# A softplus whose VectorE operations keep one operand in the matmul's PSUM bank

## The chip, the cores and the metric

The kernel runs on one core of a Trainium2 chip. The metric is the device time of one execution in microseconds (us). The engines have their own in-order instruction queues: TensorE (PE, its weight loads PEld), VectorE (DVE), ScalarE (ACT), GpSimd (POOL) and SyncE (SP). Data lies in SBUF and in eight PSUM banks, each as large as one 128 x 512 float32 tile.

## The reference

Three layers follow one another on 24576 rows (8 batches of 3072) of 256 channels: a long convolution by FFT, a first layer of 8 experts with a fixed capacity for each, and a dense second layer. The change touches the activation of the second layer alone:

```
h = x @ w_in                                        # 24576 x 256 by 256 x 2048
g = np.maximum(h, 0.0) + np.log1p(np.exp(-np.abs(h)))
return (g @ w_out).astype(np.float32)               # by 2048 x 256
```

The kernel keeps float32 accuracy: it writes each operand of a matmul as a high part, rounded to the type that the matmul reads (`F32R`), and a low part, the rest. For the same reason the logarithm is not taken as it stands. With a = exp(-|h|) and u = 1 + a rounded to float32, log1p(a) is ln(u) + (a - (u - 1)): the last term gives back what the rounding of u lost, to first order.

## The kernel before

About the first 700 us are the convolution and the first piece of the routing. After it one stage holds both layers and the rest of the routing. The 24576 rows are cut into 48 groups of 512 rows, six for each expert, and the stage is a list `seq` of steps that is written out by hand: a step of kind "m" is `moe1(i, f)`, one 128-wide slice of the expert's hidden layer, a step of kind "s" is `sp1(i, f)`, one 128-wide slice f of the second layer, called a block below. A group has 8 m steps and 16 s steps, and they alternate as m, s, s. The recording order is the order on each engine; no scheduler moves anything.

In each step PE does 12 matmuls of 128 x 512: six for the step's own product into a fresh PSUM bank (`bank()`, the tile `work`), then six of an earlier step's second product (`moe2` two steps later, `sp2` four steps later), which add up in four more banks `y` and `o`. So four banks are left for `work`, and these also take transposes and the small matmuls of the routing.

A block goes through several engines. `sp1` records on ACT a = |h| (L982), a = exp(-a) (L983), l = ln(1 + a) (L986); on DVE p = max(h, 0) + a (L984) and a = (a + 1) - 1 (L987); on POOL l = l - a (L989). `join`, called within the next step, adds p to l on DVE (L997), and `split`, called within the step after, rounds the sum to gh on ACT (L1004) and subtracts it on POOL to get gl (L1006). Of the m steps the names are hh (ACT, L949) and hl (DVE, L950). The bank of a block is last read by p; a, p and l lie in SBUF, three buffers each.

DVE has a second job. `Router` decides which row goes to which expert, one expert at a time (a phase), while the groups of the expert before are computed. `advance` records a piece of it at the head of a step, ahead of the step's own DVE work: preparing keys (L171 to L202), 16 rounds of a bisection, each with three counting passes over 1536 columns (L220) and a few operations on 3 columns (L223, L229, L232), and index lists at the end (L366 to L396). A phase takes 144 steps, six times 24. After the last phase the groups run without routing. The weights of the next expert are split by L788 and L793 on DVE. POOL issues the indirect DMAs (L766, L775, L918, L1047).

## Time and profile before

| | |
|---|---|
| time, median of 3 runs | 4475.76 us (4472.63 to 4477.92) |
| profiled execution, span | 4480.6 us |
| busy share PE / DVE / ACT / POOL | 92% / 88% / 57% / 65% |
| chain that ended last, by engine | DVE 42%, PE 42%, POOL 5%, issue 4%, ACT 3% |

The profiled execution is given by its span, from the first to the last instruction; it lies 4.8 us above the median of the three timed runs. Two engines share the chain evenly. The span has to be read by stages: in the page's 40 slices DVE is at eight or nine tenths from the eighth to the 32nd and at six to eight behind that, where the routing is over and PE is at nine to the last but one.

### The profile page before, as it was taken

What the parts mean: (1) busy time and instruction counts of PE and PEld (TensorE: products, weight loads), DVE (VectorE), ACT (ScalarE), POOL (GpSimd) and SP (SyncE); (2) the same over time, 40 slices, a digit from 0 to 9 for tenths busy, and PEclk for the clock granted to TensorE, in tenths of its full rate; (3) what the DMA queues carried; (4) which work ended last, traced back from release to release, by engine and by line L of the source; (5) the groups of instructions that cost most, each with busy time, mean ns of one, the idle gap of its engine ahead of it and who ended that gap; (6) DMA issues with size and microseconds to landing.
All of it is one profiled execution on the core that took longest, in us unless ns stands there. A gap on an engine that the chain in (4) does not pass through costs nothing.

```text
span 4480.6 us, 57930 instructions
## 1 busy us (share of the span) xinstructions
PE 4109.7 (92%) x19372; PEld 3273.8 (73%) x19372; DVE 3940.3 (88%) x6302; ACT 2575.1 (57%) x4749; POOL 2932.6 (65%) x2627
## 2 busy tenths in 40 slices
PE   8999888889889988899889988998889999999998
PEld 7898766667666766677667766776667788778886
DVE  6999666999999899999999999999998987787776
ACT  4565554445555555555555655565555666666665
POOL 3444334557666776677666866777668777887776
PEclk9999989999999999999999999999999999999999
DMA  9888660000000010000000000001000000000000
GB/s 270 260 256 245 189 170 27 10 12 24 29 13 16 20 32 15 10 24 28 16 16 11 29 26 11 17 20 34 12 10 25 23 20 14 24 27 14 20 12 12
DMA packets 226491, 228.87 MB, mean 51 GB/s; under 512 B 19376, under 2 KB 183600, under 8 KB 226192
## 3 DMA queue, kind: packets, MB, share of 16 engines
q1 hardware_dynamic: 195056, 144.25, 11.3%
q0 software_dynamic: 26528, 72.53, 5.1%
q10 hardware_dynamic: 4608, 8.39, 0.6%
q8 instruction: 153, 2.51, 0.2%
q14 instruction: 146, 1.20, 0.1%
HBM read 125.74 MB, written 93.85 MB: 49 GB/s over the span
## 4 chain that ended last, share of the span: by engine, by line
DVE 42%; PE 42%; POOL 5%; issue 4%; ACT 3%; DMA 2%; DVEq 0%; SPq 0%; another core or an unknown queue 0%; ACTq 0%; POOLq 0%
PE work L976 11%; PE o L1018 11%; DVE U L220 10%; DVE l L997 6%; PE work L945 6%; PE y L960 6%; DVE a L987 5%; DVE p L984 4%; POOL l L989 3%; DVE hl L950 2%; PE bank L669 2%; DVE c L232 2%; PE bank L583 1%; PE pair L604 1%; DVE U L202 1%
## 5 line engine op out<-in xcount | busy, mean ns | idle before, releaser
L989 POOL TENSOR_TENSOR l<-l,a 128x512 f32<-128x512 f32 x768 | 1135.3, 1478 | 617.6 <-DVE a L987 591.5
L1006 POOL TENSOR_TENSOR gl<-l,gh 128x512 fp32r<-128x512 f32 x760 | 1002.5, 1319 | 404.9 <-ACT gh L1004 399.5
L976 PE MATMUL work<-yh,WI 128*128 128x512 f32 x3072 | 876.7, 407 | 57.6 <-DVE hl L950 38.3
L1018 PE MATMUL o<-gh,WO 128*128 128x512 f32 x3072 | 869.9, 404 | 64.9 <-DVE oT L1023 39.0
L1004 ACT CAST gh<-l 128x512 fp32r<-128x512 f32 x768 | 473.1, 616 | 751.2 <-DVE l L997 744.5
L997 DVE TENSOR_TENSOR l<-l,p 128x512 f32<-128x512 f32 x768 | 743.4, 968 | 69.0 <-POOL l L989 65.6
L976 PEld LDWEIGHTS work<-yh,WI 128*128 128x128 f32 x3072 | 567.7, 191 | 268.1 <-DVE hl L950 63.3
L1018 PEld LDWEIGHTS o<-gh,WO 128*128 128x128 f32 x3072 | 585.1, 192 | 229.4 <-DVE oT L1023 48.6
L987 DVE TENSOR_SCALAR a<-a 128x512 f32<-128x512 f32 x768 | 606.0, 789 | 140.3 <-ACT l L986 75.8
L982 ACT ACTIVATE a<-work 128x512 f32<-128x512 f32 x768 | 452.6, 589 | 322.1 <-PE work L976 311.6
L220 DVE TENSOR_SCALAR_CACHE_REDUCE U<-U,c 128x1536 bf16<-128x1536 uint16 x336 | 607.6, 1808 | 12.7 <-DMA raw<-w_in 7.1
L984 DVE SCALAR_TENSOR_TENSOR p<-work,a 128x512 f32<-128x512 f32 x768 | 525.0, 684 | 98.0 <-ACT a L983 91.6
L1018 PE MATMUL o<-gl,WO 128*128 128x512 f32 x1536 | 499.2, 406 | 48.4 <-POOL gl L1006 31.2
L986 ACT ACTIVATE l<-a 128x512 f32<-128x512 f32 x768 | 483.9, 630 | 36.4 <-ACT a L983 1.8
L976 PE MATMUL work<-yl,WI 128*128 128x512 f32 x1536 | 497.2, 404 | 5.5 <-DVE yl L967 4.4
L983 ACT ACTIVATE a<-a 128x512 f32<-128x512 f32 x768 | 485.7, 632 | 24.4
L949 ACT ACTIVATE hh<-work 128x512 fp32r<-128x512 f32 x384 | 229.4, 597 | 366.3 <-PE work L945 364.9
L945 PE MATMUL work<-xh,wring 128*128 128x512 f32 x1536 | 433.5, 404 | 4.3 <-DVE p L984 4.1
L960 PE MATMUL y<-hh,wring 128*128 128x512 f32 x1536 | 430.6, 403 | 0.0
L1018 PEld LDWEIGHTS o<-gl,WO 128*128 128x128 f32 x1536 | 287.4, 191 | 148.0 <-POOL gl L1006 55.5
L976 PEld LDWEIGHTS work<-yl,WI 128*128 128x128 f32 x1536 | 293.8, 191 | 85.5 <-DVE yl L967 14.4
L960 PEld LDWEIGHTS y<-hh,wring 128*128 128x128 f32 x1536 | 296.1, 193 | 73.3
(233 smaller groups left out, 6018.0 us busy)
## 6 DMA issues: line engine op xcount, KB each, us to landing
x<-x SPq DMA_DIRECT2D x96, 256.0 KB
a_cols<-a SPq DMA_DIRECT2D x96, 256.0 KB
A<-a_cols SPq DMA_DIRECT2D x64, 384.0 KB
y_rows<-yo SPq DMA_DIRECT2D x128, 192.0 KB
f_late<-U SPq DMA_DIRECT2D x72, 192.0 KB
YT<-f_late SPq DMA_DIRECT2D x72, 192.0 KB
U<-U SPq DMA_DIRECT2D x48, 96.0 KB
raw<-moe_w_in ACTq DMA_DIRECT2D x16, 256.0 KB
```

The source lines that it names most:

```text
L220: V.tensor_scalar(s, R, c3[:, k:k + 1], 0.0, op0=OP.is_ge, op1=OP.add, accum_out=cnt[:, k:k + 1])
L945: nc.tensor.matmul(b, w[:, wh, k], xx[i][:, k], start=(n == 0), stop=(n == 5))
L960: nc.tensor.matmul(Yb[i][m], w[:, 1, wh, m * 128:(m + 1) * 128], hx, start=(f == 0 and n == 0), stop=(f == 7 and n == 2))
L976: nc.tensor.matmul(b, WI[:, wh, k, f * 128:(f + 1) * 128], yy[i][:, k], start=(n == 0), stop=(n == 5))
L983: nc.scalar.activation(a, a, AF.Exp, scale=-1.0)
L984: nc.vector.scalar_tensor_tensor(p, b, 0.0, a, op0=OP.max, op1=OP.add)
L986: nc.scalar.activation(l, a, AF.Ln, bias=1.0)
L987: nc.vector.tensor_scalar(a, a, 1.0, -1.0, op0=OP.add, op1=OP.add)
L989: nc.gpsimd.tensor_tensor(l, l, a, op=OP.subtract)
L997: nc.vector.tensor_tensor(l, l, p, op=OP.add)
L1006: (nc.vector if i == NT - 1 and f % 2 else nc.gpsimd).tensor_tensor(gl, l, gh.bitcast(F32), op=OP.subtract)
L1018: nc.tensor.matmul(Ob[i][m], WO[:, wh, f, m * 128:(m + 1) * 128], gx, start=(f == 0 and n == 0), stop=(f == 15 and n == 2))
```

## The change

The tile p is gone, a tile u takes its place. ACT writes u = 1 + a and takes the logarithm of u. All VectorE work of the block moves into `join`: three operations, of which the first two write their result into the block's PSUM bank, and the third, into SBUF, reads it from there. First h becomes max(h, 0) + ln(u), then (u - 1) minus that, then a minus that: the same sum, ln(u) + max(h, 0) + (a - (u - 1)). POOL loses its subtraction and keeps gl.

```diff
             a = wk.tile([128, 512], F32, name="a", bufs=3)
-            p = wk.tile([128, 512], F32, name="p", bufs=3)
+            u = wk.tile([128, 512], F32, name="u", bufs=3)
             l = wk.tile([128, 512], F32, name="l", bufs=3)
             nc.scalar.activation(a, b, AF.Abs)
             nc.scalar.activation(a, a, AF.Exp, scale=-1.0)
-            nc.vector.scalar_tensor_tensor(p, b, 0.0, a, op0=OP.max, op1=OP.add)
+            nc.scalar.activation(u, a, AF.Identity, bias=1.0)
             split(0)
-            nc.scalar.activation(l, a, AF.Ln, bias=1.0)
-            nc.vector.tensor_scalar(a, a, 1.0, -1.0, op0=OP.add, op1=OP.add)
+            nc.scalar.activation(l, u, AF.Ln)
             join(0)
-            nc.gpsimd.tensor_tensor(l, l, a, op=OP.subtract)
-            joins.append((i, f, l, p))
+            joins.append((i, f, b, a, u, l))
...
         def join(keep):
             while len(joins) > keep:
-                i, f, l, p = joins.pop(0)
-                nc.vector.tensor_tensor(l, l, p, op=OP.add)
+                i, f, b, a, u, l = joins.pop(0)
+                nc.vector.scalar_tensor_tensor(b, b, 0.0, l, op0=OP.max, op1=OP.add)
+                nc.vector.scalar_tensor_tensor(b, u, -1.0, b, op0=OP.add, op1=OP.subtract)
+                nc.vector.tensor_tensor(l, a, b, op=OP.subtract)
                 parts.append((i, f, l))
```

The line numbers of the changed kernel are u = 1 + a L984, the logarithm L986, and L995, L996, L997 for the three operations of `join`; L1004 and L1006 stay gh and gl.

On DVE, in a bisection of a routing phase (the end of one round and the start of the next, where a group of 512 rows ends and the next begins; U is the routing's scratch, c its thresholds), these rows stood:

```order
L220 TENSOR_SCALAR U_21895,cnt<-U_21785,c_22009 128x1536
L223 SCALAR_TENSOR_TENSOR low<-rconst,c_22009 128x3
L984 SCALAR_TENSOR_TENSOR p<-work,a 128x512
L987 TENSOR_SCALAR a<-a 128x512
L997 TENSOR_TENSOR l<-l,p 128x512
L950 SCALAR_TENSOR_TENSOR hl<-work,hh 128x512
L997 TENSOR_TENSOR l<-l,p 128x512
L933 TENSOR_TENSOR xl<-work,xh 128x512 x2
L229 TENSOR_SCALAR ge,n<-work 128x3
L232 SCALAR_TENSOR_TENSOR c_22133<-n,low 128x3
L220 TENSOR_SCALAR U_21895,cnt<-U_21785,c_22133 128x1536
```

and these stand at the same place now:

```order
L220 TENSOR_SCALAR U_21893,cnt<-U_21785,c_22007 128x1536 x2
L223 SCALAR_TENSOR_TENSOR low<-rconst,c_22007 128x3
L995 SCALAR_TENSOR_TENSOR work<-work,l 128x512
L996 SCALAR_TENSOR_TENSOR work<-u,work 128x512
L997 TENSOR_TENSOR l<-a,work 128x512
L950 SCALAR_TENSOR_TENSOR hl<-work,hh 128x512
L995 SCALAR_TENSOR_TENSOR work<-work,l 128x512
L996 SCALAR_TENSOR_TENSOR work<-u,work 128x512
L997 TENSOR_TENSOR l<-a,work 128x512
L933 TENSOR_TENSOR xl<-work,xh 128x512 x2
L229 TENSOR_SCALAR ge,n<-work 128x3
L232 SCALAR_TENSOR_TENSOR c_22133<-n,low 128x3
```

The two operations of a block's own step (p and a) are gone, and the three of `join` stand where L997 alone stood, in the next step: the first of two s steps in a row records none of this on DVE any more.

On ACT, the rows of an m step and the two s steps behind it stood so (the last row is the next m step's):

```order
L949 ACTIVATE hh<-work 128x512
L1004 CAST gh<-l 128x512
L982 ACTIVATE a<-work 128x512
L983 ACTIVATE a<-a 128x512
L1004 CAST gh<-l 128x512
L986 ACTIVATE l<-a 128x512
L982 ACTIVATE a<-work 128x512
L983 ACTIVATE a<-a 128x512
L986 ACTIVATE l<-a 128x512
L949 ACTIVATE hh<-work 128x512
```

and so now:

```order
L949 ACTIVATE hh<-work 128x512
L1004 CAST gh<-l 128x512
L982 ACTIVATE a<-work 128x512
L983 ACTIVATE a<-a 128x512
L984 ACTIVATE u<-a 128x512
L1004 CAST gh<-l 128x512
L986 ACTIVATE l<-u 128x512
L982 ACTIVATE a<-work 128x512
L983 ACTIVATE a<-a 128x512
L984 ACTIVATE u<-a 128x512
L986 ACTIVATE l<-u 128x512
```

Each s step has one operation more (L984), ahead of the logarithm. The order on PE is unchanged.

One more thing moves. The pool of the four `work` banks gives a new tile the bank that was given back first in the recorded order. Before, that made the banks take turns, each new tile taking that of the fourth tile before it, for each of the 1543 tiles but the first four. A block now gives its bank back after the third operation of `join`, a step later, and the built program has other pairs: 32 of its tiles take the bank of a block two steps back or two and a half (15 that of a first s block, 17 that of a second one), and another 48, which are transposes in the main, that of a first s block two and a half steps back. All others wait for a block's bank from three to five steps back, or for one that something else held.

## Rows read from the trace of the kernel before

**Rows 1.** Page, part 1: busy us (share of the span), instructions of each engine.

```profile
PE 4109.7 (92%) x19372; PEld 3273.8 (73%) x19372; DVE 3940.3 (88%) x6302; ACT 2575.1 (57%) x4749; POOL 2932.6 (65%) x2627
```

**Rows 2.** Windows over a 144-step phase: busy us of PE, PEld, DVE, ACT, POOL; clock.

```profile
2519.00:2598.00 79.00, 70.93 (x303) 54.37 (x301) 77.15 (x101) 46.74 (x87) 60.88 (x50) 1.00 0.12 34
2598.00:2849.00 251.00, 222.02 (x928) 171.11 (x928) 238.74 (x357) 138.60 (x243) 164.86 (x137) 0.97 0.05 15
2849.00:2925.00 76.00, 71.90 (x326) 56.90 (x326) 71.03 (x128) 45.06 (x78) 54.19 (x44) 1.00 0.04 15
2925.00:2999.00 74.00, 73.23 (x339) 57.55 (x339) 65.31 (x124) 45.56 (x79) 59.92 (x51) 1.00 0.08 26
```

**Rows 3.** Windows, 24 steps behind the last phase, same columns.

```profile
4100.00:4169.00 69.00, 69.00 (x306) 55.65 (x305) 53.76 (x63) 44.54 (x79) 52.83 (x44) 1.00 0.05 16
```

**Rows 4.** Lines in 2519 to 2999: xcount, busy us, mean ns, idle before, its releasers.

```profile
L989 POOL TENSOR_TENSOR l<-l,a 128x512 f32<-128x512 f32 x96 | 142.6, 1486 | 83.5 <-DVE a L987 80.8 <-DVE ge L229 1.4 <-PE work L226 0.5
L1006 POOL TENSOR_TENSOR gl<-l,gh 128x512 fp32r<-128x512 f32 x96 | 128.1, 1335 | 44.9 <-ACT gh L1004 44.2
...
L997 DVE TENSOR_TENSOR l<-l,p 128x512 f32<-128x512 f32 x97 | 89.0, 918 | 7.6 <-POOL l L989 6.7 <-POOL spacer L1046 0.6
...
L987 DVE TENSOR_SCALAR a<-a 128x512 f32<-128x512 f32 x96 | 67.1, 699 | 16.6 <-ACT l L986 7.7 <-DVE p L984 0.5
L984 DVE SCALAR_TENSOR_TENSOR p<-work,a 128x512 f32<-128x512 f32 x96 | 65.4, 681 | 1.2 <-ACT a L983 1.1
...
L986 ACT ACTIVATE l<-a 128x512 f32<-128x512 f32 x96 | 60.5, 630 | 5.0 <-ACT a L983 0.4 <-issue 0.4
...
L788 DVE TENSOR_TENSOR wring<-raw,wring 128x256 fp32r<-128x256 f32 x8 | 13.9, 1744 | 0.0
...
L232 DVE SCALAR_TENSOR_TENSOR c<-n,low 128x3 f32<-128x3 f32 x14 | 13.5, 963 | 0.5
```

**Rows 5.** Window of the bisection, L987 alone: its busy us and count.

```profile
2598.00:2849.00 251.00, 29.01 (x48) 0.97 0.05 15
```

**Rows 6.** The same of L997 alone.

```profile
2598.00:2849.00 251.00, 41.55 (x49) 0.97 0.05 15
```

**Rows 7.** Single lines in 2519 to 2999: ns, shortest/median/longest.

```profile
L987 DVE TENSOR_SCALAR a<-a x96: 426/428/2211, 2521.0 to 2994.9; 128x512 f32<-128x512 f32 x96
L997 DVE TENSOR_TENSOR l<-l,p x97: 675/684/2453, 2517.3 to 2997.5; 128x512 f32<-128x512 f32 x97
L232 DVE SCALAR_TENSOR_TENSOR c<-n,low x14: 161/1070/1287, 2629.9 to 2835.7; 128x3 f32<-128x3 f32 x14
L788 DVE TENSOR_TENSOR wring<-raw,wring x8: 412/1422/3352, 2558.4 to 2634.2; 128x256 fp32r<-128x256 f32 x8
```

**Rows 8.** Timeline, a bisection: start us, us, engine and line.

```profile
2643.19 0.08 DVE L229 DVE_READ_ACCUMULATOR ge<-work 128x1 f32 x1
2643.31 0.16 DVE L232 SCALAR_TENSOR_TENSOR c<-n,low 128x3 f32<-128x3 f32 x1
2643.51 1.81 DVE L220 TENSOR_SCALAR_CACHE_REDUCE U<-U,c 128x1536 bf16<-128x1536 uint16 x1
...
2647.88 1.31 POOL L1006 TENSOR_TENSOR gl<-l,gh 128x512 fp32r<-128x512 f32 x1
...
2648.71 0.69 DVE L984 SCALAR_TENSOR_TENSOR p<-work,a 128x512 f32<-128x512 f32 x1
2649.14 1.28 POOL L989 TENSOR_TENSOR l<-l,a 128x512 f32<-128x512 f32 x1
2649.50 1.21 DVE L987 TENSOR_SCALAR a<-a 128x512 f32<-128x512 f32 x1
...
2650.64 0.68 DVE L997 TENSOR_TENSOR l<-l,p 128x512 f32<-128x512 f32 x1
```

**Rows 9.** Single lines over the whole run, columns as in rows 7.

```profile
L984 DVE SCALAR_TENSOR_TENSOR p<-work,a x768: 671/684/693, 715.7 to 4462.6; 128x512 f32<-128x512 f32 x192
```

**Rows 10.** The same of the last operation of an index list.

```profile
L396 DVE SCALAR_TENSOR_TENSOR idx<-bb,jj x24: 166/167/1854, 646.2 to 3605.4; 128x8 int32<-128x8 f32 x24
```

## The prediction

> **What bounds the kernel now.** I read the page's busy times first: PE and DVE are both near nine tenths of the span, ACT and POOL well below [rows 1]. That does not say which of the two sets the pace, so next come windows over one phase of the routing, 144 steps or six groups of 24, cut where a group begins. Keys are prepared in the first stretch (a group), the second holds the bisection (three groups), the third mixes smaller pieces, the last holds the index lists [rows 2]. DVE is busy 77.15 of 79 us in the first and 238.7 of 251 us in the bisection, while PE has room there. In the last stretch PE is busy 73.23 of 74 us and DVE 65.31. Behind the last phase the same 24 steps take 69.0 us with PE busy for all of them and DVE for 53.8 [rows 3]. So 69 us are PE's floor for 24 steps, a little more with routing matmuls between, and whatever lies above it in the first five groups (76 to 84 us against some 70) is DVE's. A change on DVE can win at most that: 480 us less about 5 times 70 and once 73.2, some 57 us a phase.
>
> Why is DVE so full? The same operation takes very different times. p, with one operand in PSUM, is the same each time (671 to 693 ns), but a (426 to 2211) and l + p (675 to 2453), which have everything in SBUF, are not, nor are the 3-column L232 (161 to 1287) and L788 (412 to 3352) [rows 7, 9]. The timeline shows what they wait for: p starts amid POOL's gl and takes its usual 0.69 us, a starts 0.36 us into POOL's l - a and ends 0.29 us behind it, at 1.21 us [rows 8]. POOL's two subtractions are busy 142.6 and 128.1 us of the 480 [rows 4], 56% of the time.
>
> **The change, part by part.** One operation on ACT more, one on POOL less, three on DVE for three, 96 blocks a phase and 768 in all.
>
> DVE, the block itself. What counts is the time from one start to the next. An operation that needs nothing of the one before starts 0.07 us ahead of its end (a at 2649.50 for 1.21, L997 at 2650.64); one that must wait for it starts 0.10 us behind (p ends at 2649.40, a starts at 2649.50), or 0.04 us behind where it waits for that alone (L232 behind L229) [rows 8]. Before, a block in the bisection costs 0.78 for p, 29.01/48 - 0.07 = 0.53 for a, 41.55/49 - 0.07 = 0.78 for L997 [rows 5, 6]: 2.09 us. In the other three groups a and L997 have the rest of their 67.1 and 89.0 us [rows 4], 0.79 and 0.99 us each, and a block costs 2.42 us. After, all three have one operand in PSUM and one in SBUF, as p has, so I give each p's 0.68 us. The second waits for the first, the third for the second and for POOL: 0.72 + 0.78 + 0.61 = 2.11 us. That is as good as nothing in the bisection and 0.31 us won for a block elsewhere. No row shows VectorE writing to PSUM. Below, the cost is bounded by handovers that cost nothing, 1.97 us. Above, by a bank that must take a read and a write in turns: 128x256 takes 0.412 us [rows 7] and 128x512 0.68, so 512 columns are 0.53 us of it and doubling them gives 1.21 us for each of the first two, 3.2 us a block. I take p's time, the nearest row, and keep the upper end as a rival.
>
> Here a rule of the Trainium skill speaks against the change. "VectorE: DVE Perf Modes", section "The perf-mode tier table", says that a float32 tensor_scalar with all operands in SBUF runs at twice the rate, and anything with a PSUM operand at the single rate: a was the cheap one of the three. The shortest rows agree with it, 426 ns for a against 671 for p [rows 7, 9]; what the mean rows say is that a seldom stays cheap here (699 ns) [rows 4]. By the shortest rows the old block costs 0.78 + 0.36 + 0.61 = 1.75 us and the new one 0.36 more. Which it is depends on POOL: a rival below.
>
> DVE, the routing's and the weights' operations. POOL keeps gl alone, 128.1 of 480 us, 27% in place of 56%. L232 lies 13.5 - 14 x 0.161 = 11.2 us above its shortest over a phase, all in the bisection, L788 13.9 - 8 x 0.412 = 10.6 us, most of it in the first stretch [rows 4, 7]. I take half off, and a little more for smaller operations like them: 7 us in the bisection, 6 in the first stretch.
>
> DVE's waits. Of 12.3 idle us in the bisection [rows 2] 4.8 are the 0.10 us behind p. The rest are waits for ACT's logarithm and POOL's l - a, 7.7 and 6.7 us over the phase [rows 4]. Both go; what comes instead is L995's wait for the logarithm of a block that is a step old, with the routing's next piece and hl queued behind it. I take half of 7.5 off, 3.7 us.
>
> ACT gets u: 630 ns, as the logarithm [rows 4], 16 times in 24 steps, 10 us on top of 44.5 to 46.7 [rows 2, 3]. It stays below 58 of 69 us, and hides. Queued behind it are gh of an earlier block and the logarithm; gl, which PE needs four steps after the block, comes 0.63 us later, with POOL free for it sooner.
>
> The bank. PE needs a bank for each step. Before, a block gave its bank back after p, some 4 us from its first matmul. Now it is 1.4 for six matmuls (a twelfth of 69/24 us each, and half of twelve), four or five ACT operations of about 0.62, three on DVE: some 6.8 us for the first s block of a pair and 8 for the second, which waits behind hl of the next step. Tiles that take it three to five steps later (8.6 us and more) don't notice. Of the 32 that come two steps or two and a half later, at 5.8 to 7 us, each may wait 0.5 to 2; I add 10 us to the span.
>
> The sum by stretches. Bisection: 0 - 7 - 3.7, 251 to 240 us. First: 79 - 0.31 x 16 - 6 = 68, where PE's floor takes over, so 70: -9. Third: 76 - 5 for the blocks and -1.7, half of its 3.4 us of waits, would be 69.3; its PE is busy 71.9, so about 70.5: -5.5. Last: PE, -0.5. Together -25.7 us a phase. From the first block at 715.7 us to the last index list at 3605.4 [rows 9, 10] there are 2890/480 = 6.0 phases' worth: -155 us. Behind that PE is full: 0. The last group has sixteen s steps in a row, five ACT operations (3.1 us) each against 2.9 on PE: +3. With the banks -142 us: a span of 4339, and since the profiled span lies 4.8 us above the median, a time of 4334 us.
>
> **The rivals.** *POOL's relief is worth more.* If the operations that wait for POOL lose not half but all of the excess, and DVE no longer waits at all, the bisection gains another 7 + 3.8 us a phase, 65 us: 4269. For it: two POOL subtractions back to back [rows 8] make the longest waits, and they no longer come in pairs. Against: gl stays.
>
> *The banks hold PE up.* If the 32 tiles wait 2 us each, and the 48 others that come 2.5 steps later another 1, it is 112 us in place of 10: 4436. For it: 6.8 and 8 us take no account of DVE's routing piece ahead of the join, up to 1.8 us for a counting pass [rows 8]. Against: where DVE is late, PE has time in hand.
>
> *Slower: writing to PSUM.* If the first two operations take 1.21 us, a block costs 1.1 us more in the bisection, 53 - 10.7 = +42 us there, and 0.8 more elsewhere, 13 us in each other stretch: the first goes to 79 + 13 - 6, the third to 76 + 13 - 1.7, the last, where DVE has 9 us in hand, to 78. That is +64 us a phase, 385 in all: 4870. It decides from about 0.17 us on each of the two: 160 such operations in the bisection, the first and the third stretch make up the 25.7 us.
>
> *Slower: a and l + p are long for another reason than POOL's subtraction*, and the routing stays as it is. Then the shortest rows count: 0.36 us a block more, +17 - 3.7 us in the bisection, +6 and +4 in the first and the third: +23 a phase, 138 us, and 13 for the banks and the end: 4630. Against it is the timeline [rows 8]. This is what the tier table of the page named above would give.
>
> *No change*: PE paces the first five groups after all, by dependencies that the windows don't show: 4476. Against: the same steps in 69.0 us [rows 3].
>
> **How the numbers follow.** Forecast 0.55 (4334, its own range 4280 to 4395); more relief 0.15; banks 0.11; PSUM writes 0.09; no POOL effect 0.05; no change 0.05. From the bounds, 4229 (more relief, with free handovers, 0.14 x 48 us a phase, 40 us) to 4436 (banks) holds the first three, 0.81. Faster by over 0.2% (9 us, about what a measurement tells): 0.55 + 0.15 + 0.11 = 0.81; same 0.05; slower 0.14.
>
> **What the profile after would show.** The three operations of the join at 0.68 us with a narrow spread; a spread of L232 and L788 that shrinks; u at 0.63 us; POOL's busy time down by some 1100 us; DVE's less than that of PE in the first stretch of a phase, 70 us long, and about 80 us for each group of the bisection; 69 us a group behind the last phase, as before. L995 or L996 above 0.9 us, or PE's first matmul of a step waiting for L997 time and again, would make the prediction wrong.

## The result and the profile after

| | before | changed |
|---|---|---|
| time, median (range) | 4475.23 us (4472.63 to 4477.92) | 4294.27 us (4287.7 to 4296.55) |
| profiled execution, span | 4480.6 us | 4293.3 us |

The ratio is 0.9585, with a 95% interval of 0.9574 to 0.9597: the change takes 181 us. The forecast was 4334 us, with a range that holds the result and an own range of the likeliest case that does too; it was 40 us too careful.

Busy time and share of each engine in the changed kernel (page, part 1; before in [rows 1]):

```profile
PE 4050.7 (94%) x19372; PEld 3255.7 (76%) x19372; DVE 3442.0 (80%) x6302; ACT 3022.9 (70%) x5517; POOL 1745.8 (41%) x1859
```

POOL's busy time is down by 1187 us, ACT's up by 448, both as the edit says. DVE has as many instructions as before and 498 us less to do: that is where the time comes from. The same four stretches of a phase as in [rows 2], cut at the same steps, and the 24 steps of [rows 3]:

```profile
2394.87:2465.87 71.00, 69.22 (x303) 54.93 (x301) 61.26 (x100) 56.33 (x103) 35.64 (x34) 1.00 0.13 38
2465.87:2705.55 239.68, 219.87 (x931) 171.87 (x931) 223.27 (x363) 166.61 (x290) 90.30 (x88) 0.97 0.05 16
2705.55:2778.89 73.34, 72.10 (x325) 57.37 (x325) 53.90 (x123) 53.77 (x94) 28.88 (x28) 0.98 0.05 15
2778.89:2851.80 72.91, 72.57 (x339) 57.44 (x338) 51.84 (x122) 54.45 (x95) 36.01 (x35) 1.00 0.08 26
...
3912.20:3981.35 69.15, 69.15 (x306) 55.55 (x305) 41.70 (x62) 54.20 (x95) 28.74 (x28) 1.00 0.05 16
```

79, 251, 76 and 74 us have become 71.0, 239.7, 73.3 and 72.9; behind the last phase a group takes what it took (69.0 and 69.15), but for two (71.3 and 74.8 us before, 69.1 and 70.6 now), the second of which splits the last expert's weights. DVE is busy for 61.26 and 53.90 us where it was busy for 77.15 and 71.03: in the first and the third stretch PE is the bound now (69.22 of 71.0, 72.10 of 73.34). In the bisection DVE still is, with 223 of 240 us.

Lines in this phase (columns as in [rows 4]):

```profile
L1006 POOL TENSOR_TENSOR gl<-l,gh 128x512 fp32r<-128x512 f32 x96 | 125.9, 1311 | 253.4 <-ACT gh L1004 211.8 <-PE o L1018 24.9 <-PE work L930 13.4
L976 PE MATMUL work<-yh,WI 128*128 128x512 f32 x385 | 112.4, 414 | 10.8 <-DVE l L997 8.3 <-DVE hl L950 2.4
...
L996 DVE SCALAR_TENSOR_TENSOR work<-u,work 128x512 f32<-128x512 f32 x96 | 66.8, 696 | 3.3
L995 DVE SCALAR_TENSOR_TENSOR work<-work,l 128x512 f32<-128x512 f32 x96 | 66.4, 691 | 27.1 <-ACT l L986 27.1
L997 DVE TENSOR_TENSOR l<-a,work 128x512 f32<-128x512 f32 x96 | 66.0, 687 | 10.0
...
L945 PE MATMUL work<-xh,wring 128*128 128x512 f32 x192 | 53.7, 401 | 3.7 <-DVE l L997 3.7
...
L788 DVE TENSOR_TENSOR wring<-raw,wring 128x256 fp32r<-128x256 f32 x8 | 7.6, 946 | 3.1 <-ACT wring L787 2.0 <-ACT gh L1004 1.1
L930 PE MATMUL work<-ident,rows 128*128 128x128 f32 x48 | 7.1, 277 | 3.9 <-DVE l L997 3.9
...
L232 DVE SCALAR_TENSOR_TENSOR c<-n,low 128x3 f32<-128x3 f32 x14 | 2.3, 161 | 0.5
```

The 13.5 us of L232 are 2.3, the 13.9 of L788 are 7.6. New waits stand beside it: DVE for the logarithm (27.1 us before L995), PE for a bank that L997 gives back (8.3, 3.7 and 3.9 us). And the spread of single lines (columns as in [rows 7]; the first three of the whole run, the others of this phase):

```profile
L995 DVE SCALAR_TENSOR_TENSOR work<-work,l x768: 680/690/700, 716.6 to 4278.7; 128x512 f32<-128x512 f32 x192
L996 DVE SCALAR_TENSOR_TENSOR work<-u,work x768: 695/696/697, 717.3 to 4279.4; 128x512 f32<-128x512 f32 x192
L997 DVE TENSOR_TENSOR l<-a,work x768: 686/687/691, 718.1 to 4280.2; 128x512 f32<-128x512 f32 x192
...
L232 DVE SCALAR_TENSOR_TENSOR c<-n,low x14: 160/161/165, 2492.0 to 2688.9; 128x3 f32<-128x3 f32 x14
L788 DVE TENSOR_TENSOR wring<-raw,wring x8: 411/608/2209, 2432.6 to 2496.8; 128x256 fp32r<-128x256 f32 x8
```

2304 operations with a PSUM operand, two thirds of which write to PSUM, lie between 680 and 700 ns, while the operations that they replaced went up to 2211 and 2453 [rows 7].

### The profile page after: what moved, and what is told of

Same layout as the page of the kernel before. It is cut to its first block, busy times and chain, and to the rows that moved or that the text cites. A ratio compares the mean times of both kernels' runs of the same rounds, so it can differ in the third digit from the quotient of the medians.

```text
span 4293.3 us, 57570 instructions
## 1 busy us (share of the span) xinstructions
PE 4050.7 (94%) x19372; PEld 3255.7 (76%) x19372; DVE 3442.0 (80%) x6302; ACT 3022.9 (70%) x5517; POOL 1745.8 (41%) x1859
## 4 chain that ended last, share of the span: by engine, by line
PE 51%; DVE 29%; issue 7%; ACT 5%; POOL 4%; DMA 2%; DVEq 0%; SPq 0%; POOLq 0%; ACTq 0%
PE work L976 14%; PE o L1018 13%; DVE U L220 9%; PE work L945 8%; PE y L960 7%; DVE work L996 4%; DVE l L997 4%; DVE work L995 3%; POOL gl L1006 3%; PE bank L669 2%; DVE hl L950 2%; PE pair L604 1%; PE bank L583 1%; ACT a L983 1%; ACT u L984 1%
## 5 line engine op out<-in xcount | busy, mean ns | idle before, releaser
L1006 POOL TENSOR_TENSOR gl<-l,gh 128x512 fp32r<-128x512 f32 x760 | 992.2, 1306 | 2010.1 <-ACT gh L1004 1794.2
L976 PE MATMUL work<-yh,WI 128*128 128x512 f32 x3072 | 879.6, 408 | 84.7 <-DVE l L997 57.6
L1018 PE MATMUL o<-gh,WO 128*128 128x512 f32 x3072 | 856.4, 399 | 26.6 <-DVE oT L1023 20.1
L995 DVE SCALAR_TENSOR_TENSOR work<-work,l 128x512 f32<-128x512 f32 x768 | 531.2, 692 | 310.8 <-ACT l L986 310.1
L976 PEld LDWEIGHTS work<-yh,WI 128*128 128x128 f32 x3072 | 568.3, 191 | 249.2 <-DVE l L997 80.0
L220 DVE TENSOR_SCALAR_CACHE_REDUCE U<-U,c 128x1536 bf16<-128x1536 uint16 x336 | 608.1, 1810 | 14.8 <-DMA raw<-w_in 7.4
L997 DVE TENSOR_TENSOR l<-a,work 128x512 f32<-128x512 f32 x768 | 527.8, 687 | 82.1 <-DVE work L996 3.7
L1004 ACT CAST gh<-l 128x512 fp32r<-128x512 f32 x768 | 469.7, 612 | 163.1 <-DVE l L997 158.4
L996 DVE SCALAR_TENSOR_TENSOR work<-u,work 128x512 f32<-128x512 f32 x768 | 534.6, 696 | 26.3
L986 ACT ACTIVATE l<-u 128x512 f32<-128x512 f32 x768 | 483.8, 630 | 34.5
L984 ACT ACTIVATE u<-a 128x512 f32<-128x512 f32 x768 | 485.6, 632 | 24.5
L976 PE MATMUL work<-yl,WI 128*128 128x512 f32 x1536 | 492.2, 402 | 0.0
L1018 PE MATMUL o<-gl,WO 128*128 128x512 f32 x1536 | 485.1, 397 | 0.6 <-POOL gl L1006 0.4
L945 PE MATMUL work<-xh,wring 128*128 128x512 f32 x1536 | 431.8, 402 | 12.6 <-DVE l L997 11.5
L950 DVE SCALAR_TENSOR_TENSOR hl<-work,hh 128x512 fp32r<-128x512 f32 x384 | 263.7, 687 | 177.2 <-ACT hh L949 164.5
L976 PEld LDWEIGHTS work<-yl,WI 128*128 128x128 f32 x1536 | 293.8, 191 | 72.3
L945 PEld LDWEIGHTS work<-xh,wring 128*128 128x128 f32 x1536 | 281.7, 189 | 86.8 <-DVE l L997 15.5
L1018 PEld LDWEIGHTS o<-gl,WO 128*128 128x128 f32 x1536 | 289.5, 189 | 73.3 <-POOL gl L1006 1.9
```

The lines of the kernel that those rows point to most:

```text
L220: V.tensor_scalar(s, R, c3[:, k:k + 1], 0.0, op0=OP.is_ge, op1=OP.add, accum_out=cnt[:, k:k + 1])
L945: nc.tensor.matmul(b, w[:, wh, k], xx[i][:, k], start=(n == 0), stop=(n == 5))
L976: nc.tensor.matmul(b, WI[:, wh, k, f * 128:(f + 1) * 128], yy[i][:, k], start=(n == 0), stop=(n == 5))
L984: nc.scalar.activation(u, a, AF.Identity, bias=1.0)
L986: nc.scalar.activation(l, u, AF.Ln)
L995: nc.vector.scalar_tensor_tensor(b, b, 0.0, l, op0=OP.max, op1=OP.add)
```

## Where a DVE operation waits for POOL

Two pieces of timeline show the mechanism (start us, us, engine and line). Before, in a bisection:

```profile
2627.86 1.67 POOL L989 TENSOR_TENSOR l<-l,a 128x512 f32<-128x512 f32 x1 [0.36 <-DVE a L987]
2628.31 1.51 DVE L793 TENSOR_TENSOR wring<-raw,wring 128x256 fp32r<-128x256 f32 x1
...
2629.89 1.30 POOL L1006 TENSOR_TENSOR gl<-l,gh 128x512 fp32r<-128x512 f32 x1 [0.35 <-ACT gh L1004]
2629.93 1.27 DVE L232 SCALAR_TENSOR_TENSOR c<-n,low 128x3 f32<-128x3 f32 x1
2631.23 1.81 DVE L220 TENSOR_SCALAR_CACHE_REDUCE U<-U,c 128x1536 bf16<-128x1536 uint16 x1
```

L232 works on three columns, starts 0.04 us behind gl and ends with it (2631.20 and 2631.19). L793 starts 0.45 us into POOL's l - a and ends 0.29 us behind it. After:

```profile
2563.42 1.80 DVE L220 TENSOR_SCALAR_CACHE_REDUCE U<-U,c 128x1536 bf16<-128x1536 uint16 x1
2564.25 1.29 POOL L1006 TENSOR_TENSOR gl<-l,gh 128x512 fp32r<-128x512 f32 x1 [2.98 <-PE o L1018]
2565.15 0.09 DVE L220 DVE_READ_ACCUMULATOR U<-U,c 128x1 f16 x1
2565.15 0.69 DVE L950 SCALAR_TENSOR_TENSOR hl<-work,hh 128x512 fp32r<-128x512 f32 x1
2565.75 0.69 DVE L995 SCALAR_TENSOR_TENSOR work<-work,l 128x512 f32<-128x512 f32 x1
2566.48 0.70 DVE L996 SCALAR_TENSOR_TENSOR work<-u,work 128x512 f32<-128x512 f32 x1
```

hl, which reads work from PSUM, starts amid gl and takes its 0.69 us.

I went through the timeline of both kernels from 680 us on and took from each DVE operation the shortest of its line and shape; the rest is called its excess here (read from rows to 0.01 us; the sums are good to a few per cent). Before, operations that started while gl ran had some 0.47 us of it on average, those that started while l - a ran 0.25; those that started while POOL was idle had 0.01 us (some 1200 operations), and those in which POOL's l - a only began while they ran 0.01 (some 650). So it is the later of the two that waits. That is what the Trainium skill says in "SBUF — State Buffer", section "Who interferes with whom": a VectorE instruction with two SBUF inputs, or in a two-port mode, shares a port with GpSimd, the one issued first holds it for its whole length, and an instruction with at most one SBUF input outside those modes stays clear of it. These rows agree, with some 0.69 us (671 to 700 ns) for every 128x512 operation with a PSUM operand among them; POOL's operations in them are subtractions, with two inputs. For POOL's operation with one input, in half_pool and all_pool below, the rows do not agree: the five DVE lines with two SBUF inputs that were counted are held up in the first half us of its 1.95 alone, and not for its whole length.

Summed over all operations outside the blocks, the excess is 381 us before and 86 after: 295 us less. Of the part before, about 99 us fell on operations that started while POOL was at an indirect DMA (13 after), and nearly all of that on operations that ended only behind the subtraction that followed the DMA; so an operation can wait for more than one of POOL's. The three operations of the block are 281 us shorter in sum (1874.4 to 1593.6 us over the run), but nearly all of that lies outside the bisection: 24 steps with index lists have 33.6 in place of 43.6 us of them, 24 with keys 31.7 in place of 39.4, 24 of a bisection 33.2 in place of 33.6. Of L232, 51 of the 84 behind 680 us started within one of POOL's subtractions before, 1 after.

## Experiments

All were timed against the kernel before, in the same runs; the last column is the median less the changed kernel's 4294 us. The kernel before had medians of 4475 to 4480 us in these sets of runs, so a difference of 10 us in the last column is little above what can be told.

| kernel | time, us | ratio to before (95%) | us to the changed kernel |
|---|---|---|---|
| pool_back | 4437.40 | 0.9912 (0.9896 to 0.9929) | +143 |
| pool_sync | 4505.71 | 1.0056 (1.0039 to 1.0073) | +211 |
| sbuf_mid | 4283.89 | 0.9567 (0.9551 to 0.9583) | -10 |
| sub_dve | 4504.02 | 1.0060 (1.0044 to 1.0077) | +210 |
| no_sub | 4185.82 | 0.9350 (0.9335 to 0.9366) | -108 |
| one_op | 4080.03 | 0.9111 (0.9096 to 0.9127) | -214 |
| no_u | 4264.27 | 0.9523 (0.9507 to 0.9539) | -30 |
| shift | 4266.85 | 0.9529 (0.9514 to 0.9545) | -27 |
| half_pool | 4255.40 | 0.9506 (0.9490 to 0.9521) | -39 |
| all_pool | 4914.29 | 1.0973 (1.0954 to 1.0991) | +620 |
| mid_shift | 4275.07 | 0.9547 (0.9531 to 0.9563) | -19 |
| by_stage | 4212.36 | 0.9412 (0.9396 to 0.9428) | -82 |

The expectations weigh three theories of the gain. Share: DVE pays by the share of time in which POOL is busy with operations that read two SBUF inputs. Step: it pays because DVE itself releases POOL's subtraction and its next operation runs into it. Order: the gain came from the waits in the block's own step, which the move into `join` takes away.

A second table gives the mean length of 24 steps from 1200 us to the end of the routing (30 groups, sorted by what the routing does in them; read from the starts of ACT's L949 and first operation of a block). A group that has it behind it (no routing) takes 69.

| 24 steps, us | bisection | bisection and weights | end of bisection | index lists | keys |
|---|---|---|---|---|---|
| before | 82.9 | 88.7 | 77.4 | 77.9 | 75.0 |
| changed | 78.1 | 78.5 | 75.3 | 74.3 | 70.5 |
| pool_back | 81.6 | 85.4 | 75.7 | 76.7 | 74.1 |
| pool_sync | 81.5 | 92.6 | 80.0 | 78.3 | 76.1 |
| sub_dve | 86.6 | 84.8 | 77.5 | 76.5 | 76.2 |
| sbuf_mid | 77.4 | 76.9 | 74.4 | 73.6 | 70.6 |
| shift | 77.8 | 72.6 | 75.5 | 74.2 | 70.4 |
| mid_shift | 77.2 | 74.8 | 74.0 | 73.8 | 70.5 |
| half_pool | 74.0 | 79.8 | 72.2 | 75.1 | 71.5 |
| by_stage | 75.6 | 72.5 | 72.3 | 73.5 | 70.4 |
| one_op | 70.5 | 69.6 | 70.2 | 72.4 | 69.7 |

### POOL's second subtraction given back: pool_back and pool_sync

The changed kernel with a subtraction on POOL that nobody reads, once released by ACT's u, once by DVE's L997.

pool_back has it in `sp1`, behind `join(0)`:

```diff
+            z = wk.tile([128, 512], F32, name="z", bufs=1)
+            nc.gpsimd.tensor_tensor(z, u, a, op=OP.subtract)
```

pool_sync has it in `join`, behind L997 (both have two buffers of u in place of three, which makes room for z):

```diff
+                z = wk.tile([128, 512], F32, name="z", bufs=1)
+                nc.gpsimd.tensor_tensor(z, l, a, op=OP.subtract)
```

> The changed kernel with a subtraction of the old size put back on POOL for each block: z = u - a into a tile that nobody reads, at the place where POOL's subtraction stood, released by ACT's u (u has two buffers here in place of three). VectorE's work is unchanged. Share theory: what POOL's subtraction costs the routing's and the weights' operations on VectorE goes by the share of time that POOL is busy with two-input operations; that rises from 27% to some 55% again, so L232 goes back to a mean near 0.9 us and L788 to 1.4 or more, and the time to 4390 to 4440. Step theory: the cost came because VectorE itself released POOL (a ended, POOL's subtraction began, the next VectorE operation ran into it); a subtraction released by ACT meets VectorE by chance only, L232 stays below 0.5 us on the mean, and the time at 4295 to 4340. Order theory (the gain is that VectorE no longer waits within a block's own step, POOL has no part in it): 4294 within 10, and L232 at 0.16.

> The changed kernel with the same unread subtraction on POOL for each block, z = l - a, but recorded behind L997 in the join, so that VectorE's own third operation releases it (u has two buffers here). Share theory: as the kernel with the subtraction released by ACT, 4390 to 4440, since POOL's busy time is the same. Step theory: clearly slower than that kernel; what stands behind the join on VectorE (L220, L232, hl, the weights' L788) starts together with it, and those with two SBUF inputs wait 1.0 to 1.3 us: L232 and L788 near their old means, 4380 to 4450. Order theory: 4294 within 10.

Released by ACT, the subtraction gives 143 of the 181 us back, which is in Share's range; released by DVE it gives back all and 30 more, which is above every range. L232's mean is 0.31 us in pool_back and 0.37 in pool_sync, far below the 0.9 that Share had for the first and the old mean (0.85) that Step had for the second. In both the block itself stays as it was, as the rows of pool_sync show (lines over the whole run, columns as in [rows 4]):

```profile
L999 POOL TENSOR_TENSOR z<-l,a 128x512 f32<-128x512 f32 x768 | 1013.7, 1320 | 1024.2 <-DVE l L997 871.8 <-DVE ge L229 84.2 <-PE work L976 15.1
...
L996 DVE SCALAR_TENSOR_TENSOR work<-u,work 128x512 f32<-128x512 f32 x768 | 534.4, 696 | 26.3
L995 DVE SCALAR_TENSOR_TENSOR work<-work,l 128x512 f32<-128x512 f32 x768 | 531.3, 692 | 285.2 <-ACT l L986 285.2
...
L793 DVE TENSOR_TENSOR wring<-raw,wring 128x256 fp32r<-128x256 f32 x56 | 73.8, 1317 | 25.2 <-ACT wring L792 25.2
```

The routing's and the weights' operations pay: over the run their excess is 242 us in pool_back and 327 in pool_sync, against 86 in the changed kernel. 156 and 241 us more on DVE stand beside 143 and 211 us more of time. The two buffers of u are not what costs: ACT waits only 9 and 5 us for the join's second operation before it writes u. So most of the gain is that POOL's subtraction is gone. POOL's two 128x512 operations are as long in both runs (2002 and 2008 us), so the 68 us between them are not Share's. They are not all Step's either: in pool_sync gl stands behind z on POOL, and PE waits 83 us for gl, where it waits 7 in pool_back and 0.4 in the changed kernel. How the 68 us divide is not shown. Order falls as the main cause, since the block's steps are those of the changed kernel here; if it has a part, it lies in the 38 us that pool_back does not give back.

### The intermediate in SBUF: sbuf_mid

```diff
-                nc.vector.scalar_tensor_tensor(b, b, 0.0, l, op0=OP.max, op1=OP.add)
-                nc.vector.scalar_tensor_tensor(b, u, -1.0, b, op0=OP.add, op1=OP.subtract)
-                nc.vector.tensor_tensor(l, a, b, op=OP.subtract)
+                nc.vector.scalar_tensor_tensor(l, b, 0.0, l, op0=OP.max, op1=OP.add)
+                nc.vector.scalar_tensor_tensor(l, u, -1.0, l, op0=OP.add, op1=OP.subtract)
+                nc.vector.tensor_tensor(l, a, l, op=OP.subtract)
```

> The changed kernel with the intermediate in SBUF: the first operation reads the bank and writes l, the second and third work on l, u and a, all in SBUF; the bank is given back after the first. This undoes the part of the change that keeps an operand in PSUM. Share theory: L996 and L997 now collide with gl (27% of the time), each 0.15 to 0.25 us longer on the mean, some 5 us for a group of the bisection, against bank waits that go (PE's waits for L997, some 84 us over the whole run in the profile after): 4270 to 4330. Step theory: gl starts some 0.8 us behind L997, when the next operations are on, so L996 and L997 stay within 0.1 us of 0.69: 4230 to 4290, faster than the changed kernel by the bank waits. If PSUM as such were what wins (each operation with an SBUF pair slow whatever POOL does): 4400 or more.

```profile
L996 DVE SCALAR_TENSOR_TENSOR l<-u,l 128x512 f32<-128x512 f32 x768 | 647.7, 843 | 26.5
...
L997 DVE TENSOR_TENSOR l<-a,l 128x512 f32<-128x512 f32 x768 | 538.7, 701 | 26.2
L995 DVE SCALAR_TENSOR_TENSOR l<-work,l 128x512 f32<-128x512 f32 x768 | 525.1, 684 | 243.8 <-ACT l L986 243.6
```

These are lines of the whole run. Without PSUM, L996 runs into gl (843 ns in place of 696; 112 of its 113 us above its shortest fell on executions that started within gl) and DVE's block costs 118 us more over the run (1711.5 after 1593.6, the three lines together). It is 10 us faster all the same, because the bank goes back after the first operation: PE's waits for the join's bank (in front of L976, L945 and L930) are 11 us where the changed kernel has 84. So the PSUM operand does protect, and the bank that it holds seems to cost about as much as that is worth. 4284 us lies in the ranges of Share and of Step: L996's 0.15 us more is what Share had named, L997 at 0.70 what Step had.

### The subtraction moved, or left out, in the kernel before: sub_dve and no_sub

Both drop the first of these lines from the kernel before; sub_dve alone has the second, at the head of `join`.

```diff
-            nc.gpsimd.tensor_tensor(l, l, a, op=OP.subtract)
...
+                nc.vector.tensor_tensor(l, l, a, op=OP.subtract)
```

> The kernel before with POOL's l - a moved to VectorE, at the head of the join: four VectorE operations a block (p, a, l - a, l + p), no u on ACT, the own-step operations p and a where they were. Share and step theory: without POOL's subtraction a costs 0.36 and the three others 0.78, 0.60 and 0.60 from start to start, 2.34 us a block against 2.09 to 2.42 before, and the routing loses most of its excess: 80 to 82 us a bisection group against 83.7 before and 78.6 after, 4340 to 4400. Order theory: the waits within the own step stay and a fourth operation is added: 4476 or slower.

> The kernel before without POOL's l - a, and nothing in its place: it leaves out the correction a - (u - 1) of the logarithm, while L987 still computes its half of it. Three VectorE operations a block as in the changed kernel, but a and l + p all in SBUF, p and a in the block's own step, no u on ACT, the bank given back after p. If POOL's subtraction was what made a and L997 long, they fall to near 0.43 and 0.68 us, a block costs 1.75 us from start to start (2.11 in the changed kernel), and the time is below the changed kernel's: 4150 to 4230. If they were long for another reason, or if the own-step waits are what cost: 4400 or more.

sub_dve is a clear miss: no faster than before. I had thought that a and l + p would drop to their shortest once POOL had gl alone. Lines of sub_dve over the whole run:

```profile
L997 DVE TENSOR_TENSOR l<-l,p 128x512 f32<-128x512 f32 x768 | 664.9, 866 | 26.6
L996 DVE TENSOR_TENSOR l<-l,a 128x512 f32<-128x512 f32 x768 | 609.9, 794 | 0.0
L987 DVE TENSOR_SCALAR a<-a 128x512 f32<-128x512 f32 x768 | 540.1, 703 | 140.2 <-ACT l L986 74.5 <-DVE p L984 1.9 <-ACT a L982 0.5
L984 DVE SCALAR_TENSOR_TENSOR p<-work,a 128x512 f32<-128x512 f32 x768 | 525.2, 684 | 35.6 <-ACT a L983 33.6
```

a is 703 ns, its shortest being 426, and the two joins 794 and 866. gl is enough for most of that: of a's 218 us above its shortest 129 fell on executions that started within gl and 86 on those within POOL's indirect DMAs, and of the two joins' 228 us 220 within gl. The routing is as free as in the changed kernel (excess 88 us against 86), and the fourth operation eats it: the block costs 44.0 us in 24 steps of a bisection against 33.2. no_sub tells the same without the fourth operation (l + p at 955 ns, a at 736), and is 293 us faster than before: what the subtraction on POOL costs, with all that hangs on it. Its time lies in the range, but not by the reason given there: a and l + p did not fall to 0.43 and 0.68 us.

### What the correction and u cost: one_op and no_u

one_op changes `join`:

```diff
-                nc.vector.scalar_tensor_tensor(b, b, 0.0, l, op0=OP.max, op1=OP.add)
-                nc.vector.scalar_tensor_tensor(b, u, -1.0, b, op0=OP.add, op1=OP.subtract)
-                nc.vector.tensor_tensor(l, a, b, op=OP.subtract)
+                nc.vector.scalar_tensor_tensor(l, b, 0.0, l, op0=OP.max, op1=OP.add)
```

no_u changes `sp1`, and a stands for u in `join`, so its correction is another number:

```diff
-            u = wk.tile([128, 512], F32, name="u", bufs=3)
+            u = a
...
-            nc.scalar.activation(u, a, AF.Identity, bias=1.0)
...
-            nc.scalar.activation(l, u, AF.Ln)
+            nc.scalar.activation(l, a, AF.Ln, bias=1.0)
```

> The changed kernel with one VectorE operation a block in place of three: l = max(h, 0) + ln(u), so it leaves out the correction a - (u - 1). It shows what is left to win on VectorE. If VectorE still sets the pace of the bisection (78 to 79 us a group), 1.4 us less a block and a bank that comes back earlier bring every group to PE's floor of 69 to 72 us (74.5 in the index lists): 4120 to 4180. If PE's bank or ACT sets it now: above 4230.

> The changed kernel without u on ACT: the logarithm takes a with a bias of 1 and the second VectorE operation reads a in place of u, so its correction is another number. ACT has 0.63 us less a block and the logarithm comes earlier. If u is hidden as predicted: 4294 within 10. If the longer chain (bank held longer, L995 waiting for the logarithm, 310 us of idle time ahead of it in the profile after) costs: 4240 to 4280.

With one DVE operation for a block, every group falls to 69.6 to 72.4 us, PE is busy for 98% of the span, and 4080 us, 40 below the range expected, is what PE leaves. So the changed kernel still owes DVE and the waits 214 us. u is not hidden, as I had it: without it 30 us go. DVE's idle time before the first operation of the join is 204.5 us in place of 310.8, so most of it stays without u:

```profile
L994 DVE SCALAR_TENSOR_TENSOR work<-work,l 128x512 f32<-128x512 f32 x768 | 531.2, 692 | 204.5 <-ACT l L985 175.7 <-ACT gh L1003 27.8 <-issue 0.7
```

### DVE's other operations moved away: shift and mid_shift

```diff
-                (nc.vector if e else nc.gpsimd).tensor_tensor(v[:, 1], r1, v[:, 0].bitcast(F32), op=OP.subtract)
+                nc.gpsimd.tensor_tensor(v[:, 1], r1, v[:, 0].bitcast(F32), op=OP.subtract)
...
-            copy = nc.vector.tensor_copy if half else nc.scalar.copy
+            copy = nc.scalar.copy
```

The other half of the weights likewise. mid_shift adds the three lines of sbuf_mid.

> The changed kernel with 16 operations a phase (L788, L793: the low parts of the weights) moved from VectorE to POOL, and the copy of the second half of the output rows from VectorE to ACT, one of 0.68 us a group. VectorE gets some 12 us a phase less for the weights and 4 for the copies, most of it where it sets the pace: 4230 to 4270. If POOL's two-input operations cost the routing in proportion to their time, a few us a phase come back; if ACT, at 54 to 58 us a group, is near its limit, nothing is won: 4290 or more.

> sbuf_mid (10 us faster than the changed kernel) and shift (27 us faster) together: the bank goes back after the first operation of the join, GpSimd splits the weights, ScalarE copies the output rows. If the two gains are of different waits, 4257 (4247 to 4270). If SBUF operands on both sides make the join collide with GpSimd's additional work (L996 was 0.84 us in sbuf_mid), the gains don't add: 4270 to 4285.

shift gains 27 us, in the one group where the weights come (78.5 to 72.6 us). The two gains don't add: mid_shift is 8 us slower than shift. In mid_shift the join has SBUF operands, so it runs into POOL's new work (lines of the whole run):

```profile
L996 DVE SCALAR_TENSOR_TENSOR l<-u,l 128x512 f32<-128x512 f32 x768 | 664.1, 865 | 26.5
...
L997 DVE TENSOR_TENSOR l<-a,l 128x512 f32<-128x512 f32 x768 | 560.8, 730 | 26.3
```

In shift they stay at 696 and 687 ns. This is the second of the two theories in its expectation.

### The correction on POOL: half_pool, all_pool and by_stage

```diff
-            nc.scalar.activation(u, a, AF.Identity, bias=1.0)
+            if f % 2 and i < NT - 1:
+                nc.gpsimd.tensor_scalar(u, a, 1.0, -1.0, op0=OP.add, op1=OP.add)
+                nc.gpsimd.tensor_tensor(u, a, u, op=OP.subtract)
+            else:
+                nc.scalar.activation(u, a, AF.Identity, bias=1.0)
             split(0)
-            nc.scalar.activation(l, u, AF.Ln)
+            if f % 2 and i < NT - 1:
+                nc.scalar.activation(l, a, AF.Ln, bias=1.0)
+            else:
+                nc.scalar.activation(l, u, AF.Ln)
...
-                nc.vector.scalar_tensor_tensor(b, u, -1.0, b, op0=OP.add, op1=OP.subtract)
-                nc.vector.tensor_tensor(l, a, b, op=OP.subtract)
+                if f % 2 and i < NT - 1:
+                    nc.vector.tensor_tensor(l, u, b, op=OP.add)
+                else:
+                    nc.vector.scalar_tensor_tensor(b, u, -1.0, b, op0=OP.add, op1=OP.subtract)
+                    nc.vector.tensor_tensor(l, a, b, op=OP.subtract)
```

This is half_pool, which does it for odd f; all_pool does it for every f (the last group is left as it was in both); by_stage for odd f where 0 < i < 36 and i mod 6 < 3, with the edits of shift.

> In every second block GpSimd makes the correction c = a - ((a + 1) - 1) in two operations of its own, released by ScalarE's exponential, ScalarE leaves u out there, and VectorE has two operations in place of three; only the last group stays as in the changed kernel. VectorE saves 8 operations of about 0.78 us in 24 steps, 6.2 us, which counts in the bisection and the mixed group, four groups of six: 25 us a phase, 150 in all, and u's half another 15. GpSimd gets 16 operations more in 24 steps, as many as the unread operation of pool_back, which gave 143 us back. Share theory (any busy time of GpSimd with two inputs from SBUF lengthens the routing's operations): -165 + 143, about 4270 (4250 to 4310). Step theory (only what VectorE itself releases runs into the next VectorE operation): 4130 to 4180. If the first of the two GpSimd operations, with one input, costs VectorE nothing, between them: 4200.

> The same for all blocks but the last group's. VectorE saves 12.5 us in 24 steps, enough to put the bisection and the mixed group on TensorE's floor if nothing else changes; but GpSimd then has three operations a block, 16 x 3 x 1.3 = 62 us in 24 steps, with its DMA issues about 70: it is as long as TensorE's 69. Share theory: the routing's operations wait as in the kernel before and GpSimd's lateness is added: 4350 to 4450. Step theory: 4150 to 4230, with the groups behind the routing at 70 to 74 us in place of 69.

> GpSimd's two operations for every second block as in half_pool, but only in the groups where that paid there (the bisection and the one behind it, i mod 6 below 3, up to group 35; 4 to 5 us and 3 us a group), and everything of shift in all groups (27 us, nearly all of it in the group in which the weights come). If what GpSimd's work costs is decided in the stage in which it is done, the gains add: 12 groups with 4 to 5 us and 6 with 3 us, less the 27: 4294 - 55 - 16 - 27, about 4195 (4180 to 4215). If lateness is carried from one group into the next (the groups that stay would come late, or the gain is waited away there): 4230 to 4260.

half_pool lands in Share's range by its time. POOL is busy for 70% of the span, more than before the change, and the excess is 205 us where it was 381; but Share counts operations with two inputs alone, and the longest on POOL here has one. Lines of half_pool over the run, and two of its timeline:

```profile
L985 POOL TENSOR_SCALAR u<-a 128x512 f32<-128x512 f32 x376 | 734.5, 1953 | 125.6 <-ACT a L983 122.8
...
L986 POOL TENSOR_TENSOR u<-a,u 128x512 f32<-128x512 f32 x376 | 487.2, 1296 | 31.3
...
2654.10 1.93 POOL L985 TENSOR_SCALAR u<-a 128x512 f32<-128x512 f32 x1 [0.39 <-ACT a L983]
...
2655.16 0.16 DVE L232 SCALAR_TENSOR_TENSOR c<-n,low 128x3 f32<-128x3 f32 x1
```

L232 starts 1.06 us into L985, with 0.87 us of it left, and takes its 0.16 us. In half_pool and all_pool together 43 L232 started within L985 and had 0.04 us of excess on average; 70 started within one of POOL's subtractions and had 0.36. Taking L202, L223, L788 and L793 with it, which have two SBUF inputs too, 128 operations started more than half a us into L985 and lost at most 0.014 us; the 68 that started earlier lost 0.33 on average and at most 0.49. Of all DVE's operations 1696 started more than half a us into L985; they lost 0.013 us on average, and the few long ones (up to 0.49) are all but one tensor_scalars and casts. So the premise of the third case in half_pool's expectation nearly holds, POOL's operation with one input costs DVE little, though its 4200 us did not come.

In all_pool POOL is busy for 85% and the excess is 183 us. What decides between Share and its rivals is POOL's time in 128x512 operations with two inputs: it is 2138 us before with 381 of excess, 2008 in pool_sync with 327, 2002 in pool_back with 242, 1948 in all_pool with 183, 1480 in half_pool with 205 and 992 in the changed kernel with 86. So this time matters, and at nearly the same time, in the three runs around 2000 us, the excess differs by what starts within it. all_pool is slow for another reason, which I had priced too low: POOL's operation with one input takes 1.95 us, not the 1.3 of its subtraction, so a block needs 1.95 + 1.29 + 1.29 = 4.5 us of POOL, 72.5 us in 24 steps, and with the DMA issues POOL is the bound in every group (lines of all_pool):

```profile
L985 POOL TENSOR_SCALAR u<-a 128x512 f32<-128x512 f32 x752 | 1474.1, 1960 | 114.3 <-ACT a L983 103.6
...
L1028 PE MATMUL o<-gl,WO 128*128 128x512 f32 x1536 | 534.6, 430 | 433.8 <-POOL gl L1016 419.6 <-POOL spacer L1056 10.3
...
L1004 DVE TENSOR_TENSOR l<-u,work 128x512 f32<-128x512 f32 x752 | 517.3, 688 | 1469.2 <-POOL u L986 1439.3 <-POOL spacer L1056 19.7 <-DVE work L1002 0.5
```

by_stage puts POOL's work where half_pool gained by it, and is the fastest of the kernels here that keep the correction: 4212 us, 5.9% below the kernel before and 82 us below the changed one, inside the range for gains that add. It is 17 us above that expectation's middle, as the bisection's groups fell to 75.6 us and not to 74.0: the groups of the table begin eight steps ahead of those that i counts, so that a third of every second one of them kept all of its DVE work.

## Why the prediction was right, and where it was off

**The bound.** Right. DVE set the pace in the first three stretches, PE behind the routing, and PE's floor is what two of them have reached.

**The block.** Right. It was to cost as much in the bisection (2.11 us after 2.09): start to start it is 0.73 + 0.80 + 0.60 = 2.13 us, and the three lines are busy for 100.1 us in the bisection, after 103.3 (29.01 and 41.55 [rows 5, 6], and 48 times 681 ns for p [rows 4]). Outside the bisection it was to get shorter by 0.31 us, 5 us in the 16 blocks of 24 steps, and did by 7.7 with keys. Writing to PSUM is as cheap as p was (692 and 696 ns): the rival at 4870 falls. The Trainium skill's rule in "VectorE: DVE Perf Modes", section "The perf-mode tier table", that a float32 tensor_scalar is at its fast rate only with all operands in SBUF, agrees with the shortest executions of a (426 ns). But "a seldom stays cheap" is a wrong reading of a mean: the median of the phase is 428 ns [rows 7], and 55 of its 96 executions, 347 of all 768, took no more than 450. The mean of 699 comes from the long ones, and by means the old block was no shorter; with gl alone a's mean is still 703 ns (sub_dve) and 736 (no_sub).

**The routing's operations.** Right in its mechanism, too small in size: this is the term that was off. "I take half off": of L232 all went (963 ns to 161), of L788 half (1744 to 946), and of the whole excess 295 of 381 us, more than three quarters. In the bisection DVE's other operations fell from 135.4 to 123.2 us (238.7 and 223.3 less the block), 12 where the forecast had 7. The rival "POOL's relief is worth more" had this half right, and its 4269 us lies nearer to the 4294 measured than the forecast's 4334. The rival without an effect of POOL falls: pool_back puts the subtraction back and loses 143 us. What had to be counted is not only the share of time that POOL keeps, but which operations start while it runs. gl comes behind gh, which comes behind the join; of the DVE operations that start within it now, most are L995 and L996, which are immune, and L220, at 1.81 us in both kernels. l - a came behind DVE's own a, and among those that started within it were the 43 L232.

**DVE's waits.** Wrong in sign: 3.7 us were to go in the bisection. Idle time there rose from 12.3 to 16.4 us (251 less 238.74, 239.68 less 223.27), 8 us against the forecast, in part because the logarithm is later by u. That u "hides" is the step that failed: no_u puts 30 us on it. The larger part of the wait for the logarithm, 204.5 of 310.8 us over the run, is there without u. In the bisection the two errors, 5 us more from the routing and 8 less from the waits, and 3 from the block, nearly cancel, and the 240 us that were forecast came as 239.7; that it came so close is luck.

**The other stretches.** 71.0 for 70, 72.9 for 73.5; the third came to 73.3 in place of 70.5. There I went below PE's own busy time of 71.9 us [rows 2], which nothing in the change shortens. Over the phase -23.1 us for -25.7.

**The whole.** The forecast took 6.0 times this one phase, and there lies most of the 40 us that it fell short. Windows over the first three phases before (144 steps each from 687.8 us on, columns as in [rows 2]):

```profile
687.80:1200.10 512.30, 449.72 (x1868) 344.61 (x1868) 465.62 (x737) 264.29 (x463) 311.31 (x255) 0.95 0.06 19
1200.10:1696.50 496.40, 447.48 (x1899) 344.90 (x1899) 468.25 (x720) 276.39 (x486) 338.67 (x281) 0.97 0.06 19
1696.50:2183.30 486.80, 444.40 (x1897) 344.26 (x1895) 454.17 (x712) 275.03 (x485) 338.61 (x281) 0.97 0.06 20
```

and after:

```profile
687.60:1158.90 471.30, 436.88 (x1868) 341.44 (x1867) 410.31 (x735) 316.74 (x553) 177.22 (x166) 0.97 0.07 21
1158.90:1617.20 458.30, 434.96 (x1896) 339.42 (x1896) 401.12 (x722) 332.32 (x580) 190.12 (x185) 0.99 0.07 21
1617.20:2069.10 451.90, 429.92 (x1894) 337.12 (x1894) 397.74 (x713) 331.84 (x581) 190.72 (x187) 1.00 0.07 21
```

They gain 41.0, 38.1 and 34.9 us; the three behind them 24.3, 23.5 and 20.4. Six times 23.1 is 139, the six together are 182. Another 6 us, where the forecast had none, come behind the last phase, most of it from two groups (71.3 and 74.8 us before, 69.1 and 70.6 now). In the early ones PE's busy time falls too, by 12.5 to 14.5 us each (by 4.5 to 6.7 in the later ones), and the granted clock, a mean of stretches at 2.4 GHz (1.00) and at 1.2 GHz, rises from 0.95 to 0.97 in the first, with PE idle for 63 us of it before and 34 after, and to 0.99 and 1.00 in the two others. That is about half as much as they gain beyond the later ones; whether it is the cause, and what makes the rest, was not tried and stays open.

**The banks.** 10 us were set down for them. PE waits 84 us for a bank that L997 gives back, in 90 waits: "time and again", which the prediction named as a sign of being wrong, so that this term was too small. sbuf_mid, which gives it back earlier, gains 10 us net, with 118 us more on DVE. What the hold alone costs stays open between these. The last group takes 98.4 us from its first step to the end, after 98.0: 0.4 us more, for 3 forecast.

## What to carry to other kernels

Look for operations whose shortest time lies far below their mean and their longest (a median can hide it: a's was 428 ns with a mean of 699), and read in the timeline what they start behind: a three-column VectorE operation that takes 1.27 us is waiting for GpSimd, and the cure is a PSUM operand, or that GpSimd's work lies where only PSUM operands start. Count the gain by which operations start within GpSimd's two-input ones, and not by GpSimd's busy share alone: 2008, 2002 and 1948 us of these went with 327, 242 and 183 us of excess. And scale a gain from one phase to the whole only after windows over all phases: the first gained twice the last.

## Not expected of the hardware

- Of the two, VectorE's operation is lengthened only if it comes second: one within which GpSimd's l - a began had 0.01 us of excess (some 650 operations), as one with GpSimd idle had (some 1200).
- GpSimd's float32 operation with one input and two constants is slower than its subtraction of two tiles of the same size, 1.95 us against 1.30, and yet holds VectorE up less: in half_pool and all_pool the operations that started more than half a us into it lost 0.013 us on average (1696).
- VectorE writes a 128x512 result into the bank that it reads in 692 and 696 ns, and into SBUF from PSUM in 671 to 693 (p) or 687.
